# Decay tables with a per-partition factor, a merged state product, a gated first weight and a last expert by itself, in a fused RWKV and soft-MoE kernel

## The chip, the core and the metric

The kernel runs on one core of one Trainium2 chip. The metric is the device time of one execution in microseconds (us), and the median over several runs is compared. All positions in time below count from the start of the span of one profiled execution.

## What is computed

Two layers follow each other. The first is a linear attention with decay (RWKV-5): for 4 batches, 8 heads, 768 time steps and a head size of 48.

```
state = zeros(B, H, D, D)
for t in range(S):
    kt, vt, rt = k[:, :, t], v[:, :, t], r[:, :, t]
    cur = einsum('bhd,bhe->bhde', u * kt, vt)
    y[:, :, t] = einsum('bhd,bhde->bhe', rt, state + cur)
    state = w[:, :, None] * state + einsum('bhd,bhe->bhde', kt, vt)
```

Its output, as 3072 tokens of 384 features, goes through a soft mixture of 8 experts with 4 slots each (hidden size 1024):

```
logits = x @ phi                        # 3072 x 32
slot_input = softmax(logits, axis=0).T @ x
slot_out[e] = relu(slot_input[e] @ w1[e]) @ w2[e]
out = softmax(logits, axis=1) @ slot_out
```

## The kernel before, in words

**Decay.** The recurrence is turned into products of blocks of time. k and r are multiplied with tables of powers of the decay w: `W[0]` for k, `W[1]` for r, each 128 partitions x (4 head pairs q, 6 steps j, 96). An entry is exp(factor x ln w), where the factor depends on partition and j alone (`sk`, `sr`, 128 x 6) and ln w on the feature (`lnw`). `spread` (L173) copies the row w to all partitions with a matmul and takes Ln on ScalarE; `tt` (L180) multiplies `lnw` with the factor on VectorE, 576 wide; `ex` (L185) takes Exp on ScalarE. Of the four head pairs, q=0 and q=1 are made ahead of the loop (L188 to L196), q=2 and q=3 in its first steps by the table `T_AT` (L467). In the same start, GpSimd loads w and u into `wu` with two small DMAs (L107, L108), TensorE transposes it (L210), and `ucol` and `wT` come out of it (L213 to L217); nine matmuls on zeros (`keep_warm`, L137) keep TensorE busy in between.

**The loop.** The work is 16 units m (batch and head pair), each in two halves of time: 32 steps i, from -5 on with a fill (L493). The order of every engine's instructions is the order in which this loop emits them, and nothing is reordered afterwards. For one step the functions are: `a_pe` (k times r, L299) and `mask_f` (VectorE, AT, L304); `prod_f` (VectorE, L257, every second step); `y_pe` (outputs into PSUM Yb, L355 to L368) and `y_evac` (ScalarE, `x`, L375); `v_pe`/`v_evac` (v brought into order of time, L284, L290); `m_pe` (the states, into PSUM Mb, L314 to L329) and `z_evac` (VectorE: the states masked to their own head, `Z`, L343, in every even step also the state that is carried to the next half and multiplied with its decay, `Z0`, L339, and `dv`, L345); `scale` (GpSimd, the products with the decay tables, `kr`, L228, three units ahead, three buffers); `t_pe`, `t_evac` (transposes of `kr`, L235, and their ScalarE copies `kT`, `rT`, L241); `b_pe`, `b_evac` (transposed back, L247, and VectorE's copy `kn`, L252); `v_cast` (ScalarE, L270). From step 8 on `route` adds the routing of the batch before: logits (L383, L390, L399), their exponentials (L405) and the sums for the slots (L425).

**Transfers.** SP's queue carries w, then k, r and v by batch; three raw buffers hold four batches, so batch 3 is loaded into the first one again (L538). GpSimd's queue carries the expert weights, which are converted to bf16 on the way: eight of w1 (L131) and eight of w2 (L134), the last w2 in three pieces. `W_AT` (L466) says after which steps they are issued; each takes its place behind that step's GpSimd product.

**The experts.** After the loop the last two groups' logits are finished (L558 to L571), `uns` holds the slot inputs, and the first product (L594) uses four column groups of TensorE at once, one per expert. ReLU, transposes (L617) and the second product (L627) follow: for each of two expert groups g, eight blocks y, two halves x and four experts j. Its result is scaled by the column sums into `so` (L631, L632). The row sums of the second softmax (`row_sums`, L606, 24 small matmuls in all, each call with a reciprocal) stand partly ahead of, partly behind that product. Then 24 matmuls of 384 columns (L646) give the output rows, VectorE and ScalarE evacuate them in turn (L648, L650), and SP's and GpSimd's queues store them in pieces of 1, 1, 2, 4, 4, 4, 4 and 4 rows (L652).

Of the kernel before, what the change touches and what calls it, by code (L numbers as in the profile page):

```python
# [9 lines left out]
def kernel(  # L10
# [86 lines left out]
    one_f = early[0:1, 2 * H * D:2 * H * D + 128]  # L97
    warm = LexpT[:, 2048:2560]
    wu = cst.tile([8, 128], f32, name="wu")
    wu3 = wu[:].rearrange("q (e s) -> q e s", s=64)  # L100
    phi_f = cst.tile([128, nM, ES], f32, name="phi_f")
    O(act.preload_act_table_set("natural_log_exp_and_others"))
    O(sp.dma_start(out=w_row, in_=w.rearrange("(o h) d -> o (h d)", o=1)))
    O(dve.memset(wu[:], 1.0))
    O(dve.memset(warm, 0.0))
    O(dve.memset(one_f, 1.0))
    O(pool.dma_start(out=wu3[0:4, :, 0:D], in_=w.rearrange("(q e) d -> q e d", e=2)))  # L107
    O(pool.dma_start(out=wu3[4:8, :, 0:D], in_=u.rearrange("(q e) d -> q e d", e=2)))  # L108

# [7 lines left out]

    def load_batch(b, step):
        for h0 in range(0, H, step):
            load_kr(0, k, b, h0, h0 + step)  # L120
            load_kr(1, r, b, h0, h0 + step)
            load_v(b, h0, h0 + step)

    load_batch(0, 2)
    load_batch(1, 2)
    O(sp.dma_start(out=phi_f[:], in_=moe_phi.rearrange("(mo p) s -> p mo s", p=128)))
    load_batch(2, H)
# [9 lines left out]
    def keep_warm(n, bank=Yb, data=None):  # L137
        data = warm if data is None else data
        for _ in range(n):
# [4 lines left out]
    O(pool.iota(s_i, pattern=[[-1, J]], base=T - 1, channel_multiplier=-J))  # L144
    ident_f = cst.tile([128, 128], f32, name="ident_f")
    O(pool.memset(ident_f[:], 0.0))
    O(pool.affine_select(out=ident_f[:], in_=ident_f[:], compare_op=ALU.not_equal, fill=1.0, base=0,
                         pattern=[[-1, 128]], channel_multiplier=1))
# [19 lines left out]
    ident = cst.tile([128, 128], bf, name="ident")  # L168
    O(dve.tensor_copy(ident[:], ident_f[:]))

# [5 lines left out]

    spread(Xb, 0, P2)
    W = [cst.tile([128, nQ, J, P2], f32, name=f"W{j}") for j in range(2)]

# [7 lines left out]

    tt(0, 0)  # L188
    tt(1, 0)
    spread(Vb, P2, H * D)  # L190
    ex(0, 0)
    ex(1, 0)
    tt(0, 1)
    tt(1, 1)
    ex(0, 1)
    ex(1, 1)  # L196
    bmask = cst.tile([128, P2], f32, name="bmask")
    ones = cst.tile([128, 128], bf, name="ones")
    ucol = cst.tile([128, nQ, 2], bf, name="ucol")
    Le_t = [cst.tile([128, L, 128], bf, name=f"Le{j}") for j in range(2)]  # L200
    uns = cst.tile([128, nM, 2, EG, 32], bf, name="uns")
    O(pool.memset(bmask[:], 0.0))
    O(pool.memset(bmask[0:64, 0:D], 1.0))
    O(pool.memset(bmask[64:128, D:P2], 1.0))
    O(pool.memset(ones[:], 1.0))
    O(pool.memset(ucol[:], 0.0))
    for t in Le_t:
        O(pool.memset(t[:], 0.0))
    O(pool.memset(uns[:], 0.0))
    O(pe.transpose(Mb[:, 0:8], wu[:], ident_f[0:8, 0:8]))  # L210
    wuT = cst.tile([128, 8], f32, name="wuT")
    O(dve.tensor_copy(wuT[:], Mb[:, 0:8]))
    O(pool.tensor_mul(ucol[0:64, :, 0], wuT[0:64, 0:4], wuT[0:64, 4:8]))  # L213
    O(pool.tensor_mul(ucol[64:128, :, 1], wuT[64:128, 0:4], wuT[64:128, 4:8]))
    wT = cst.tile([128, nQ], f32, name="wT")
    O(act.activation(out=wT[:], in_=wuT[:, 0:4], func=AF.Ln))
    O(act.activation(out=wT[:], in_=wT[:], func=AF.Exp, scale=float(T)))  # L217
    phi_s = cst.tile([128, nM, ES], bf, name="phi_s")
    acc = cst.tile([128, NA], f32, name="acc")
    st = {}  # L220

# [110 lines left out]
    def z_evac(i):  # L332
        m, b, q, g, n = at(i)
        dv = wk.tile([128, L * 2, D], bf, name="dv", bufs=2)
        st["dv", i] = dv
        if g == 0:
            Z0 = wk.tile([128, P2], bf, name="Z0", bufs=2)
            st["Z0", m] = Z0
            O(dve.scalar_tensor_tensor(out=Z0[:], in0=Mb[:, 2 * P2:3 * P2], scalar=wT[:, q:q + 1],  # L339
                                       in1=bmask[:], op0=ALU.mult, op1=ALU.mult))  # L340
        Z = wk.tile([128, 2, P2], bf, name="Z", bufs=2)
        st["Z", i] = Z
        O(dve.tensor_mul(Z[:], Mb[:, 0:2 * P2].rearrange("p (c e) -> p c e", c=2),  # L343
                         bmask[:, None, :].to_broadcast([128, 2, P2])))
        O(dve.tensor_mul(dv[:], st["v", i][:].rearrange("p c e d -> p (c e) d"),  # L345
                         Mb[:, 288:288 + 2 * L, None].to_broadcast([128, L * 2, D])))

    def y_pe(i):
# [9 lines left out]
        for c in range(L):  # L358
            if c == 0:
                if g == 0:  # L360
                    continue
                z = st["Z0", m][:]
            else:
                z = Z[:, c - 1, :]
            t = slice((g * L + c) * C, (g * L + c + 1) * C)
            O(pe.matmul(Yb[:, c * P2:(c + 1) * P2], rT[:, t], z, start=False, stop=False,  # L366
                        skip_group_check=True))
# [24 lines left out]
    def xt_ev(n, c, xt=None, eng=None):  # L392
        xT = wk.tile([128, Dm], bf, name="xT", bufs=4)
        st["xT", n, c] = xT
        xt = xT_p if xt is None else xt
        if eng is dve:
            O(dve.tensor_copy(xT[:], xt))
        else:
            O(act.copy(xT[:], xt))  # L399
# [40 lines left out]
    def route(i, part):  # L440
# [22 lines left out]
        if s < 2 * L:  # L463
            xt_ev(*ch[s])

    W_AT = {13: 1, 14: 1, 15: 1, 16: 1, 18: 1, 19: 1, 21: 1, 22: 1, 23: 1, 25: 1, 26: 5}  # L466
    T_AT = {-4: [(dve, 0, 2), (dve, 1, 2), (act, 0, 2)], -3: [(act, 1, 2), (dve, 0, 3)],  # L467
            -2: [(act, 0, 3)], -1: [(dve, 1, 3), (act, 1, 3)]}
    nw = 0
    n0, n1 = nG - 2, nG - 1  # L470
    Wf = [t[:].rearrange("p q j d -> p (q j d)") for t in W]
    xs = Wf[0].bitcast(bf)[:, 2 * F:2 * F + 2 * L * Dm].rearrange("p (n m c t) -> p n m c t", n=2, m=nM, c=L)

# [19 lines left out]
    for i in range(-5, nH):  # L493
# [39 lines left out]
        if i == nH - 3:  # L533
            turn(n1, (0, 1), T1, act)
        for eng, j, q in T_AT.get(i, ()):
            (tt if eng is dve else ex)(j, q)
        if i == 3:
            load_batch(3, H)  # L538
        if i == 4:
            for mi in range(nM):  # L540
                O(dve.tensor_copy(phi_s[:, mi, :].rearrange("p (j g s) -> p g j s", g=2, s=Spe),
                                  phi_f[:, mi, :].rearrange("p (g j s) -> p g j s", g=2, s=Spe)))
        for _ in range(W_AT.get(i, 0)):
# [62 lines left out]
    def row_sums(a, z):  # L606
        for i in range(a, z):
            O(pe.matmul(Mb[:, i:i + 1], LexpT[:, i:Nn:nN], ones[:, 0:1],
                        start=(i == a), stop=(i == z - 1), skip_group_check=True))
        O(dve.reciprocal(rsr[:, a:z], Mb[:, a:z]))  # L610

# [3 lines left out]
    for g in range(2):  # L615
# [4 lines left out]
        if g == 0:  # L620
            row_sums(0, 8)
    SO = [Xb[:, 0:HD], Yb[:, 0:HD]]
    for g in range(2):
        for y in range(nF):
            for x in range(2):
                for j in range(EG):
                    O(pe.matmul(SO[x][32 * j:32 * j + 32, :], hT[g][:, y, 32 * j:32 * j + 32],  # L627
                                w2_of(g * EG + j)[:, y, x * HD:(x + 1) * HD],
                                start=(g == 0 and y == 0), stop=(g == 1 and y == nF - 1), skip_group_check=True))
    so = cst.tile([128, Dm], bf, name="so")  # L630
    O(dve.tensor_scalar_mul(so[:, 0:HD], SO[0], csr[:, 0:1]))  # L631
    O(act.activation(out=so[:, HD:Dm], in_=SO[1], func=AF.Copy, scale=csr[:, 0:1]))  # L632
    row_sums(8, 16)

    out_v = out.rearrange("(p n) m -> p n m", n=nN)
    ob = [T1[:].bitcast(f32), T0[:].bitcast(f32), Ab0, Vb[:], Xb[:], Yb[:]]
    sizes = [1, 1, 2, 4, 4, 4, 4, 4]
    obuf = ([raw[0][:, 16 * Dm:17 * Dm], raw[0][:, 17 * Dm:18 * Dm], Wf[0][:, 0:2 * Dm], Wf[1][:, 0:4 * Dm]]
            + [raw[0][:, x * 4 * Dm:(x + 1) * 4 * Dm] for x in range(4)])
    i = 0  # L640
    for gi, sz in enumerate(sizes):
        o_s = obuf[gi][:, 0:sz * Dm].rearrange("p (n m) -> p n m", m=Dm)
        i0 = i
        for j in range(sz):
            op = ob[i % 6][:, 0:Dm]
            O(pe.matmul(op, LexpT[:, i:Nn:nN], so[:], start=True, stop=True))  # L646
            if i % 2 == 0:
                O(dve.tensor_scalar_mul(o_s[:, j, :], op, rsr[:, i:i + 1]))  # L648
            else:
                O(act.activation(out=o_s[:, j, :], in_=op, func=AF.Copy, scale=rsr[:, i:i + 1]))  # L650
            i += 1
        O((sp, pool)[gi % 2 if gi > 1 else 0].dma_start(out=out_v[:, i0:i, :], in_=o_s))  # L652
        if gi == 2:
            row_sums(16, nN)

# [29 lines left out]
```

## Time and profile before

| | |
|---|---|
| runs | 125.37 us median of 3 (124.92 to 125.81) |
| profiled execution | 124.32 us, span 122.5 us, mean granted TensorE clock 0.967 |
| busy | TensorE 100.0, VectorE 97.3, ScalarE 84.2, GpSimd 62.5 us |
| DMA | 31.79 MB in all; mean 259 GB/s over the span |
| main loop | until about 94 us |
| first product of the experts starts | 98.27 us |
| second product | 102.54 us to 105.3 us |
| `so` complete | 105.84 us |
| first output store issued | 106.93 us |
| last GpSimd output store issued | 113.38 us |

A busy time is the sum of an engine's instructions; matmuls are pipelined and their ends modelled, so TensorE's is high without the engine being at its peak. An instruction's duration is longer than the distance to the next one's start, as neighbours overlap: two VectorE products of 0.95 us follow each other after 0.87 us. In lines of the timeline the columns are start, duration, engine, line, operation, output and inputs, count, and in brackets idle time ahead and what ended it. In lines of groups the columns after the bar are busy time and mean duration in ns, then idle time ahead.

### The profile page before, as it was taken

How to read it: one execution, taken by the hardware profiler on the slowest of the kernel's cores; microseconds unless marked ns; L12 is line 12 of the kernel's file. 1: busy time of each engine (PE TensorE's matmuls, PEld its weight loads, DVE VectorE, ACT ScalarE, POOL GpSimd, SP SyncE). 2: the span in 40 equal slices, each digit the busy share in tenths (PEclk: the TensorE clock that was granted, in tenths of full speed). 3: DMA queues.
4: the chain of work that ended last, by engine and by line, in shares of the span. 5: the costliest groups of instructions: out<-in, count | busy, mean ns of one | idle time of the engine just before them, and what ended most of it. 6: DMA issues, size and time to landing. Idle time of an engine off the chain costs nothing.

```text
span 122.5 us, 4329 instructions
## 1 busy us (share of the span) xinstructions
PE 100.0 (82%) x1784; PEld 80.5 (66%) x1785; DVE 97.3 (79%) x200; ACT 84.2 (69%) x176; POOL 62.5 (51%) x75
## 2 busy tenths in 40 slices
PE   5698988898898998989899898999979799994000
PEld 1356866686687877979778797777878549962000
DVE  1998899999999999899999999999978235598000
ACT  4479768777868798886889887788858253397000
POOL 5899999995756778494687758110000000011100
PEclk9999999999999999999999999999999999999655
DMA  2999999999999999999999999999999992069992
GB/s 66 290 372 374 372 372 366 347 388 362 328 384 372 324 217 215 212 219 212 217 218 211 220 209 215 216 217 218 215 214 215 210 193 49 5 235 395 401 415 94
DMA packets 21093, 31.79 MB, mean 259 GB/s; under 512 B 1361, under 2 KB 18258, under 8 KB 21074
## 3 DMA queue, kind: packets, MB, share of 16 engines
q0 software_dynamic: 3088, 14.95, 55.1%
q1 hardware_dynamic: 17986, 16.57, 40.1%
q8 instruction: 14, 0.23, 0.7%
q14 instruction: 5, 0.04, 0.1%
HBM read 39.38 MB, written 4.72 MB: 360 GB/s over the span
## 4 chain that ended last, share of the span: by engine, by line
DVE 38%; PE 31%; issue 11%; POOL 7%; ACT 4%; DVEq 1%; POOLq 1%; ACTq 0%
DVE prod L257 11%; DVE AT L304 8%; DVE dv L345 6%; DVE Z L343 5%; PE Vb L284 5%; DVE raw L648 3%; PE Mb L325 3%; PE Yb L368 3%; PE T L235 3%; PE T L425 2%; PE T L247 2%; POOL kr L228 2%; PE Ab L299 1%; DVE kn L252 1%; ACT W L484 1%
## 5 line engine op out<-in xcount | busy, mean ns | idle before, releaser
L228 POOL TENSOR_TENSOR kr<-raw,W 128x576 bf16<-128x576 f32 x30 | 43.2, 1459 | 14.6 <-PE T L235 11.1
L304 DVE TENSOR_TENSOR AT<-Ab,mask_ut 128x768 bf16<-128x768 f32 x32 | 30.4, 950 | 1.0 <-PE Ab L299 1.0
L284 PEld LDWEIGHTS <-Q 128*128 128x128 bf16 x288 | 16.2, 100 | 3.6 <-issue 2.9
L284 PE MATMUL Vb<-v_bf,Q 128*128 128x96 bf16 x288 | 18.2, 211 | 0.0
L235 PE MATMUL T<-ident,kr 128*128 128x128 bf16 x192 | 17.0, 230 | 0.2 <-POOL kr L228 0.2
L241 ACT COPY rT<-T 128x768 bf16<-128x768 bf16 x16 | 12.8, 798 | 6.0 <-PE T L235 2.7
L241 ACT COPY kT<-T 128x768 bf16<-128x768 bf16 x16 | 12.8, 799 | 5.1 <-PE T L235 4.8
L257 DVE TENSOR_TENSOR prod<-T,kT 128x768 bf16<-128x768 bf16 x16 | 15.1, 947 | 0.0
L375 ACT CAST x<-Yb 128x288 bf16<-128x288 f32 x32 | 13.1, 410 | 2.8 <-PE Yb L368 2.8
L652 POOL DMA_DIRECT2D out_dram<-W x1 | 0.5, 541 | 27.2 <-ACT raw L650 27.2
L345 DVE TENSOR_TENSOR dv<-vn,Mb 128x288 bf16<-128x288 bf16 x32 | 14.2, 444 | 0.0
L366 PE MATMUL Yb<-Z,rT 128*128 128x96 bf16 x80 | 10.5, 204 | 3.8 <-DVE Z L343 3.8
L290 ACT CAST vn<-Vb 128x288 bf16<-128x288 f32 x32 | 13.1, 409 | 0.5
L235 PEld LDWEIGHTS <-kr 128*128 128x128 bf16 x192 | 12.6, 102 | 1.1 <-DVE kr L228 0.5
L299 PE MATMUL Ab<-rT,kT 64*128 64x128 bf16 x192 | 11.1, 222 | 0.6 <-DVE AT L304 0.5
L325 PE MATMUL Mb<-vn,kn 128*128 128x96 bf16 (+2 forms) x80 | 11.5, 243 | 0.0
L343 DVE TENSOR_TENSOR Z<-Mb,bmask 128x192 bf16<-128x192 f32 x32 | 11.1, 347 | 0.0
L355 PE MATMUL Yb<-vn,AT 128*128 128x48 bf16 x192 | 10.3, 185 | 0.0
L368 PE MATMUL Yb<-dv,ident 128*128 128x288 bf16 x32 | 9.1, 284 | 1.4
L270 ACT CAST v_bf<-raw 128x576 bf16<-128x576 f32 x15 | 10.1, 676 | 0.0
L252 DVE COPY kn<-T 128x768 bf16<-128x768 bf16 x16 | 8.9, 555 | 1.4 <-PE T L247 0.7
L355 PEld LDWEIGHTS <-AT 128*128 128x128 bf16 x192 | 6.9, 96 | 3.2
(141 smaller groups left out, 209.4 us busy)
## 6 DMA issues: line engine op xcount, KB each, us to landing
w_all<-in_moe_w_dram POOLq DMA_DIRECT2D x8, 768.0 KB, 10.3
raw<-in_moe_w_dram POOLq DMA_DIRECT2D x7, 768.0 KB, 14.7
raw<-in_k_dram SPq DMA_DIRECT2D x8, 288.0 KB, 6.1
raw<-in_r_dram SPq DMA_DIRECT2D x8, 288.0 KB, 6.0
raw<-in_v_dram SPq DMA_DIRECT2D x8, 288.0 KB, 6.1
raw<-in_k_dram SPq DMA_DIRECT2D x2, 1152.0 KB, 10.9
raw<-in_r_dram SPq DMA_DIRECT2D x2, 1152.0 KB, 9.9
raw<-in_v_dram SPq DMA_DIRECT2D x2, 1152.0 KB, 13.1
```

The costliest lines, as they stand in the source:

```text
L228: O(eng.tensor_mul(kr[:, j].rearrange("p j (h s) -> p j h s", s=64)[:, :, :, 0:D], src, W[j][:, q].rearrange("p j (h d) -> p j h d", h=2)))
L235: O(pe.transpose(bank[:, x * C:(x + 1) * C], kr[:, j, x, :], ident[:]))
L241: O(act.copy(t[:].rearrange("p (s j) -> p s j", j=J), bank[:, 0:S].rearrange("p (j s) -> p s j", j=J)))
L257: O(dve.tensor_mul(pr[:].rearrange("p (s j) -> p s j", j=J), T1[:, 0:S].rearrange("p (j s) -> p s j", j=J), st["kT", m][:].rearrange("p (s ...
L284: O(pe.matmul(Vb[:, c * P2:(c + 1) * P2], Q3[:, o:o + C], vb[:, :, g, j, :], start=(j == 0), stop=(j == JV - 1)))
L290: O(act.copy(vn[:].rearrange("p c e d -> p (c e d)"), Vb[:, 0:L * P2]))
L304: O(dve.tensor_mul(AT[:], Ab[:, :, 0:T].rearrange("p e (c t) -> p e c t", c=L), mask_ut[:, None, None, :].to_broadcast([128, 2, L, C])))
L325: O(pe.matmul(o, kn[:, g * L + c, :], vc, start=first, stop=True, skip_group_check=True))
L343: O(dve.tensor_mul(Z[:], Mb[:, 0:2 * P2].rearrange("p (c e) -> p c e", c=2), bmask[:, None, :].to_broadcast([128, 2, P2])))
L345: O(dve.tensor_mul(dv[:], st["v", i][:].rearrange("p c e d -> p (c e) d"), Mb[:, 288:288 + 2 * L, None].to_broadcast([128, L * 2, D])))
L355: O(pe.matmul(Yb[:, o:o + D], AT[:, e, c, :], vn[:, c, e, :], start=first, stop=False, skip_group_check=True))
L375: O(act.copy(st["x", n][:, :, q * P2:(q + 1) * P2], Yb[:, 0:L * P2].rearrange("p (c e) -> p c e", c=L)))
```

## The change

- **Decay tables.** For q=0, q=2 and q=3 a new function `ad` makes a table on ScalarE alone: six Exp instructions of 128 x 96, each reading `lnw` with one column of `sk` or `sr` as its factor per partition. For q=1 the product and the Exp stay, now inside the loop's fill. The tables for q=2 and q=3 come later than before (steps -2 to 1).
- **Start.** The two small DMAs into `wu` go from GpSimd's queue to ScalarE's, ahead of its table load; `wu`'s transpose stands ahead of the second `spread`; `ucol`'s two products go from GpSimd to VectorE. Memsets of `ones` and `Le` go to step 2, that of `uns` to step 28. `ident_f` and `phi_f` lie in unused columns of `LexpT`; `xT` has two buffers for four.
- **States.** A table `zt` holds the mask for two states and, for the third, mask times decay. `Z0` is then part of `Z`: one product of 288 columns in even steps.
- **phi.** The three copies of phi go from VectorE (step 4) to ScalarE (steps 3, 4, 5).
- **Weights.** The first weights are issued in step 15 (two) for step 13 (one), behind a GpSimd copy of one column, `guard`, that reads the first part of batch 3's v; that v is loaded in two DMAs, of six heads and two.
- **Experts.** All row sums from 8 on stand ahead of the second group's product; that product is split into three experts and the last one, with two and three warm-up matmuls ahead of the parts.
- **Output.** The first two rows are evacuated in halves by both engines; the pieces are 1, 1, 2, 2, 2, 4, 4, 4 and 4 rows.

```diff
+    O(act.dma_start(out=wu3[0:4, :, 0:D], in_=w.rearrange("(q e) d -> q e d", e=2)))
+    O(act.dma_start(out=wu3[4:8, :, 0:D], in_=u.rearrange("(q e) d -> q e d", e=2)))
     O(act.preload_act_table_set("natural_log_exp_and_others"))
...
-    O(pool.dma_start(out=wu3[0:4, :, 0:D], in_=w.rearrange("(q e) d -> q e d", e=2)))
-    O(pool.dma_start(out=wu3[4:8, :, 0:D], in_=u.rearrange("(q e) d -> q e d", e=2)))
+    zt = cst.tile([128, nQ, 3, P2], f32, name="zt")
+    O(dve.memset(zt[:], 0.0))
...
+    def ad(j, q):
+        e = (sk, sr)[j]
+        for x in range(J):
+            O(act.activation(out=W[j][:, q, x, :], in_=lnw[:, q * P2:(q + 1) * P2], func=AF.Exp,
+                             scale=e[:, x:x + 1]))
+
+    ad(0, 0)
     spread(Vb, P2, H * D)
+    ad(1, 0)
...
+        O(dve.tensor_mul(Z[:], Mb[:, 0:x * P2].rearrange("p (c e) -> p c e", c=x), zt[:, q, 0:x, :]))
...
-    W_AT = {13: 1, 14: 1, 15: 1, 16: 1, 18: 1, 19: 1, 21: 1, 22: 1, 23: 1, 25: 1, 26: 5}
-    T_AT = {-4: [(dve, 0, 2), (dve, 1, 2), (act, 0, 2)], -3: [(act, 1, 2), (dve, 0, 3)],
-            -2: [(act, 0, 3)], -1: [(dve, 1, 3), (act, 1, 3)]}
+    W_AT = {15: 2, 16: 1, 18: 1, 19: 1, 21: 1, 22: 1, 23: 1, 24: 1, 25: 1, 26: 5}
+    T_AT = {-5: [(tt, 0, 1), (ex, 0, 1)], -4: [(tt, 1, 1)], -3: [(ex, 1, 1)], -2: [(ad, 0, 2)],
+            -1: [(ad, 1, 2)], 0: [(ad, 0, 3)], 1: [(ad, 1, 3)]}
...
+        if i == min(W_AT):
+            O(pool.tensor_copy(guard[:], raw_of(2, B - 1)[:, 0:1]))
...
+    second(0, range(EG))
+    row_sums(8, nN)
+    row_recip(8, nN)
+    busy(2)
+    second(1, range(EG - 1))
+    busy(3)
+    second(1, (EG - 1,))
...
-    sizes = [1, 1, 2, 4, 4, 4, 4, 4]
+    sizes = [1, 1, 2, 2, 2, 4, 4, 4, 4]
```

## The prediction

> **What bounds the kernel now.** I read the page's slices first, then DMA by windows, then VectorE, TensorE and GpSimd in order of time, and last the groups for the prices.
>
> ```profile
> DVE  1998899999999999899999999999978235598000
> ...
> DMA  2999999999999999999999999999999992069992
> GB/s 66 290 372 374 372 372 366 347 388 362 328 384 372 324 217 215 212 219 212 217 218 211 220 209 215 216 217 218 215 214 215 210 193 49 5 235 395 401 415 94
> ```
>
> Two things are full at once. VectorE is full to 90 us. DMA is full from 3 us: inputs at 370 GB/s to slice 13, then the cast weights at 215 GB/s until slice 33, a hole of four microseconds, then the output at 400 GB/s. The windows show the three joints:
>
> ```profile
> 41.50:42.00 0.50, 0.50 (x2) 1.00 1.41 351
> 42.00:42.50 0.50, 0.50 (x1) 1.00 1.03 242
> 43.50:44.00 0.50, 0.50 (x1) 1.00 1.01 210
> ...
> 103.25:103.50 0.25, 0.00 (x0) 1.00 0.04 6
> ...
> 107.75:108.00 0.25, 0.00 (x0) 1.00 0.71 264
> 108.50:108.75 0.25, 0.00 (x0) 1.00 0.07 18
> 109.00:109.25 0.25, 0.02 (x1) 1.00 1.02 362
> ```
>
> (The last two columns are DMA share and GB/s.) Inputs give way to weights at about 42.1; the last weight bytes land at 103.4; the output starts at 107.7, starves at 108.5 and is full from 109.0 to 120.25. The span ends 2.25 later, at 122.5.
>
> ```profile
> 63.98 0.45 DVE L345 TENSOR_TENSOR dv<-vn,Mb 128x288 bf16<-128x288 bf16 x1
> 64.34 0.95 DVE L304 TENSOR_TENSOR AT<-Ab,mask_ut 128x768 bf16<-128x768 f32 x1
> 65.48 0.32 DVE L339 SCALAR_TENSOR_TENSOR Z<-Mb,wT,bmask 128x96 bf16<-128x96 f32 x1 [0.19 <-PE Mb L329]
> 65.72 0.35 DVE L343 TENSOR_TENSOR Z<-Mb,bmask 128x192 bf16<-128x192 f32 x1
> 65.98 0.45 DVE L345 TENSOR_TENSOR dv<-vn,Mb 128x288 bf16<-128x288 bf16 x1
> 66.49 0.56 DVE L252 COPY kn<-T 128x768 bf16<-128x768 bf16 x1
> ```
>
> The loop takes 4.98 us for two steps. `kn` starts 0.51 after `dv`, where `dv` to AT takes 0.36: it waits 0.15 for TensorE's transposes (L247, 65.88 to 66.38). The circle is therefore dv, TensorE without a gap from 64.48 to 66.38, kn, AT, prod, Z, dv. L339 is not in it while routing (L383, L390) runs; before step 8 there is no routing and `kn` follows `dv` at 0.36 (20.97 to 21.33).
>
> ```profile
> 39.48 0.62 POOL L131 DMA_DIRECT2D w_all<-in_moe_w_dram  x1
> ...
> 42.91 1.40 POOL L228 TENSOR_TENSOR kr<-raw,W 128x576 bf16<-128x576 f32 x1 [0.36 <-PE T L235]
> 44.26 0.57 POOL L131 DMA_DIRECT2D w_all<-in_moe_w_dram  x1
> ```
>
> The first weight issues at 39.48. In the changed order it stands after the product that is here at 42.91.
>
> **The sum is against the profiled execution**: 124.32 us with a span of 122.5 (1.8 lie outside); the median of the runs is 125.37, 1.05 more, so I carry the difference over to the median.
>
> **1. Start, decay tables.** Of eight VectorE products (L182) and eight Exp (L186, 128x576), two of each stay (q=1). Six tables become six ScalarE pieces of 128x96 with a factor per partition.
>
> ```profile
> L186 ACT ACTIVATE W<-W 128x576 f32<-128x576 f32 x8 | 5.5, 685 | 1.2 <-DVE W L182 1.1
> L405 ACT ACTIVATE Le<-Xb 128x96 bf16<-128x96 f32 x6 | 1.5, 255 | 0.0
> L632 ACT ACTIVATE so<-Yb,csr 128x192 bf16<-128x192 f32 x1 | 0.4, 420 | 2.4 <-PE Yb L627 2.4
> L650 ACT ACTIVATE raw<-Vb,rsr 128x384 f32<-128x384 f32 x3 | 1.8, 609 | 0.0
> ```
>
> A piece is not in the trace. Low end: 0.14 from start to start (L405, 87.42 to 87.56, no factor). High end: its whole duration, 0.34 (0.420 of L632 less 96 columns at 0.83 ns, the slope from L632 to L650's first, 0.58). L650 repeats 0.11 sooner than its duration; I take 0.34 - 0.11 = 0.23, the rows with a factor being nearest. A table is then 6 x 0.23 = 1.4 us of ScalarE for 0.58 before.
>
> [...]
>
> VectorE loses four products of 0.67 to 0.86 between 8.7 and 17; one (16.29) stands directly on the chain between kn and AT: 0.7 gained. TensorE's `wu` transpose moves ahead of the second spread (L174) and so waits for the `wu` DMAs; behind it stand that spread, its Ln, five warm-ups and the first transposes, and on VectorE the first `kr` product. These DMAs leave GpSimd (issues of 0.74 and 0.61, landing after 3.3 and 3.8) for ScalarE's queue, at 1.05 and 1.5, ahead of the table load (1.28, then ending at 3.25, before Ln at 3.91: no cost). They land between 3.9 (2.4 after the issue, as `w_row`, issued at 0.74 and used at 3.14) and 5.3 (3.8 after); before, the wait ended at 6.07. The transpose (0.24), the spread (1.2) and five warm-ups (2.3) follow, less 0.2 of overlap: from 4.2, which I take as nearer to an empty queue, the first transposes come at 7.7 for 8.36, from 5.3 at 8.8. `zt`'s memset (1152 wide; 256 take 0.27, so 1.1) lies in VectorE's idle 1.65 before 3.05; its product (0.45) and ucol's two take the place of freed products.
>
> Then ScalarE limits. From the second kT copy (11.8: 0.9 before its 12.74) to the copy x of step 2 it has four copies of 128x768 at 0.69, two casts at 0.58, six copies of 128x288 at 0.29 and four tables at 1.4: 11.3 us, and x ends at 23.2 where it ended at 22.3. The next Yb group waits for that, and its last matmul (24.29) comes 0.24 later, at 23.45: gain 0.85. If TensorE lets kT start 0.8 earlier it is 1.65; with pieces at 0.34 it is a loss of 1.8. I take **-0.9**. GpSimd's products wait for these tables but run ahead (8 without a pause from 9.9): covered.
>
> **2. Loop.** L339 merges into L343: 0.24+0.26 start to start becomes 0.36 (as dv, 288 wide). Worth 0.09 a pair where `kn` is not held by TensorE: steps 4 to 7 (0.18) and three pairs without routing later (0.27); zero elsewhere, up to 0.14 a pair (2.2) if the circle above is wrong. Three phi copies leave VectorE (28.97 to 29.38: 0.41) for ScalarE, which idles 0.4 a step. **-0.9** together; -1.5 by step 10, -1.8 at the end. xT with two buffers, tiles in unused rows, memsets later on GpSimd (1.0): nothing, behind ScalarE's and GpSimd's idle time.
>
> **3. Weights.** The guard waits for three quarters of v, behind the first product of step 15. Half-microsecond windows from 41.0 (341, 351, 242, 277, 240 GB/s) lie between 370 for inputs and 210 for weights and hold 1.25 us of inputs: alone these would drain at 42.25, and the weights' flow amounts to a start there. Three quarters of v then land at about 41.5, with stragglers at 42.1. GpSimd comes to it at 44.26 - 1.5 = 42.75; issue at 42.9. Behind it stand two issues (1.2) and a `kr` product not needed for five steps. From issue to packets: 1.4 (output: 109.23, DMA busy from 110.65) to 2.5 (first `wu` issue 1.43, data from 3.9, GpSimd's first use, which the first weight now is). Full flow from 44.3 to 45.4 instead of 42.25. DMA was full; nothing gives this back. Last weight: 103.4 + 2.05 to 3.15, or 0.7 less if the uneven ends (100.5 to 103.4) shrink: 104.75 to 106.55, I take 106.0. The last expert alone leaves four matmuls of 0.082 after it: TensorE could end at 106.45.
>
> **4. Second product.** Before it ran from 102.54 to 105.3, 32 groups of four at 0.082. Now on TensorE's queue before its end: 16 row sums (8 in 0.52: 1.05), five warm-ups (0.21: 1.07), and the last expert's 16 matmuls by themselves (1.31; 0.33 if an expert costs its share of a group). 105.3 - 1.8 + 3.4 = **106.9**, later than the weights' 106.45. That is +1.6.
>
> **5. Output.** No row sums (0.65) or reciprocal (0.21) between so and the first row, and half rows (0.42 for 0.62): the first issue comes 0.8 after so for 1.09, gain 0.3. Five small pieces fill the hole from 108.3 to 108.95 (0.65), unless the second SP issue again takes 1.07: 0.3 to 1.0, I take **-0.95**. The remaining 4.7 MB at 400 GB/s follow unchanged.
>
> Sum: +1.6 - 0.95 = **+0.65**: 125.0 for the profiled execution, 126.0 for the median.
>
> **Rivals.**
> - *A, forecast (0.5)*: 126.0; its own range is 125.0 to 127.0.
> - *B, faster (0.23)*: TensorE gets its full rate sooner. Six transposes take 0.82 at 11.88 and 0.50 from 16.96; before, an idle gap (4.9 to 6.07) parts the warm-ups, now they run through. With 2 us more in step 1, GpSimd meets the guard as v lands and packets flow at 43.75: the last weight at 104.2, TensorE's end at 104.9, so 0.4 earlier, output -1.0: 124.0. Against it: ScalarE's 11.3 us. A loop gain of 3.7 in all decides, and the weights' uneven ends must shrink too.
> - *C, slower (0.17)*: ScalarE is the bound to step 3. Pieces at 0.28 put x at 24.4: step 1 loses 0.3, the loop's whole gain is 0.6, TensorE ends at 108.1, so +2.8 - 0.95: 127.2. It decides above 0.25 a piece. For it: no covering idle time in those 11.3 us; against: L650's repeat.
> - *D, slower (0.1)*: the first weight flows at 46.3 (GpSimd late by 1 and the 2.5): last weight 107.4, so +2.55 - 0.95: 127.0.
>
> [...]
>
> **How the numbers follow.** A measurement of this kernel tells about 1% (1.25 us) from no change. Faster is B; slower C, D and the 0.05 of A above 126.6; same the rest: 0.23, 0.45, 0.32. The range 123.8 to 127.6 leaves out under 2 in 10: B's and C's far ends.
>
> **What would show it.** ScalarE without a pause from 12 to 23 and pieces 0.23 apart (step 1); `kn` still waiting for L247's successor (2); DMA idle for 1.5 to 3 us after 42, last weight at 106 (3); no TensorE wait before the last expert (4); DMA full within 1.5 us of the first output packet (5). I am wrong if TensorE waits long for the last expert, or if the loop's end moves by 3 us or not at all.

## The result, and the profile after

The changed kernel takes 128.83 us (median of 4 runs, 128.64 to 129.2) against 125.15 for the kernel before: ratio 1.0295, 95% interval 1.0238 to 1.0351. It is slower. The profiled execution takes 128.79 us with a span of 127.0 (before 122.5). Three stretches add up to the difference:

| stretch (us) | before | after | difference | predicted |
|---|---|---|---|---|
| until the first product of the experts | 98.27 | 99.70 | +1.43 | -1.8 |
| from there to the scaling of `so` | 7.06 | 11.01 | +3.95 | +3.4 |
| from there to the end of the span | 17.17 | 16.29 | -0.88 | -0.95 |
| sum | 122.5 | 127.0 | +4.5 | +0.65 |

The profiled execution of before was 0.8 to 1.05 us below its median, that of after stands at its median. About 1 us of the +4.5 is therefore that one execution; in which line it lies, one trace of the kernel before doesn't show.

The slices of the changed kernel:

```profile
DVE  6369977779999989899898898998883350189100
...
DMA  2999999999999307999999999999999999249992
GB/s 67 303 353 374 376 370 364 361 391 352 362 384 355 90 3 114 217 215 218 217 214 215 214 214 212 211 217 215 217 216 217 216 209 203 51 170 385 403 416 112
```

DMA has a hole at slices 13 to 15, where inputs give way to weights. The windows size it (the last two columns are DMA share and GB/s), and the timeline of GpSimd says why:

```profile
43.50:48.50 5.00, 4.73 (x97) 4.02 (x94) 4.62 (x9) 4.28 (x11) 3.55 (x6) 1.00 0.00 2
49.00:50.00 1.00, 0.54 (x17) 0.43 (x14) 1.00 (x3) 0.86 (x2) 1.00 (x2) 1.00 0.46 80
109.25:109.50 0.25, 0.25 (x4) 0.24 (x4) 0.00 (x0) 0.00 (x0) 0.00 (x0) 1.00 0.13 19
...
113.00:113.25 0.25, 0.25 (x2) 0.09 (x1) 0.25 (x2) 0.25 (x2) 0.00 (x0) 1.00 0.99 344
```

```profile
27.66 16.45 POOL L227 TENSOR_TENSOR kr<-raw,W 128x576 bf16<-128x576 f32 x12
44.28 1.41 POOL L227 TENSOR_TENSOR kr<-raw,W 128x576 bf16<-128x576 f32 x1 [0.18 <-PE T L234]
45.63 0.19 POOL L546 COPY guard<-raw 128x1 f32<-128x1 f32 x1
47.08 1.28 POOL L137 DMA_DIRECT2D w_all<-in_moe_w_dram  x2 [1.26 <-issue]
```

GpSimd had lost its lead: it runs twelve products without a pause up to 44.1 and comes to the guard at 45.63. The first weight flows at 48.5, and in full from 50 on (before 42.25), the last bytes land at 109.4 (before 103.4).

The second product on TensorE, from the last products of its first group on:

```profile
105.22 0.26 PE L637 MATMUL Yb<-raw,W 128*32 128x192 bf16 x4
105.41 1.28 PE L614 MATMUL Mb<-ones,LexpT 128*128 128x1 bf16 x16
106.55 0.59 PE L146 MATMUL Ab<-w_all 128*128 128x512 bf16 x2
107.07 0.26 PE L637 MATMUL Xb<-raw,W 128*32 128x192 bf16 x3
...
108.51 0.82 PE L146 MATMUL Ab<-w_all 128*128 128x512 bf16 x3
109.26 0.26 PE L637 MATMUL Xb<-raw,W 128*32 128x192 bf16 x1
...
110.51 0.25 PE L637 MATMUL Yb<-raw,W 128*32 128x192 bf16 x1
```

No line has idle time ahead of it: TensorE works through, and no wait for a weight shows. Sixteen row sums, five warm-ups and a last expert that costs as much as the three others together (1.33 us each) stand in its queue.

The steady loop, where routing runs, is unchanged:

```profile
65.36 0.44 DVE L341 TENSOR_TENSOR dv<-vn,Mb 128x288 bf16<-128x288 bf16 x1
65.72 0.95 DVE L303 TENSOR_TENSOR AT<-Ab,mask_ut 128x768 bf16<-128x768 f32 x1
66.86 0.46 DVE L340 TENSOR_TENSOR Z<-Mb,zt 128x288 bf16<-128x288 f32 x1 [0.19 <-PE Mb L328]
67.24 0.44 DVE L341 TENSOR_TENSOR dv<-vn,Mb 128x288 bf16<-128x288 bf16 x1
67.87 0.56 DVE L251 COPY kn<-T 128x768 bf16<-128x768 bf16 x1 [0.18 <-PE T L246]
...
70.33 0.44 DVE L341 TENSOR_TENSOR dv<-vn,Mb 128x288 bf16<-128x288 bf16 x1
```

Two steps take 4.97 us (before 4.98), and `kn` still waits for TensorE. The loop's +1.43 arises between the `dv` of step 2 (21.03 for 20.97) and that of step 4 (27.34 for 25.79). There ScalarE makes the tables of q=2 and q=3, six pieces a table (`ad`, L200), and TensorE waits three times for the copies `x` behind them, 2.57 us in all:

```profile
13.49 0.80 ACT L240 COPY kT<-T 128x768 bf16<-128x768 bf16 x1 [0.90 <-PE T L234]
...
20.76 1.72 ACT L200 ACTIVATE W<-LexpT,sk 128x96 f32<-128x96 f32 x6
22.36 0.40 ACT L371 CAST x<-Yb 128x288 bf16<-128x288 f32 x1
...
25.23 0.41 ACT L371 CAST x<-Yb 128x288 bf16<-128x288 f32 x1
```

```profile
19.37 0.31 PE L351 MATMUL Yb<-vn,AT 128*128 128x48 bf16 x6 [0.58 <-ACT x L371]
22.81 0.31 PE L351 MATMUL Yb<-vn,AT 128*128 128x48 bf16 x6 [1.11 <-ACT x L371]
25.68 0.31 PE L351 MATMUL Yb<-vn,AT 128*128 128x48 bf16 x6 [0.88 <-ACT x L371]
```

Up to step 2, what the freed products bring is used up: the first transposes come at 9.30 (before 8.36), and VectorE's new product for `zt` stands ahead of the first `kn` (before 11.02):

```profile
10.67 1.77 DVE L535 TENSOR_TENSOR zt<-zt,wT 128x384 f32<-128x384 f32 x1
12.36 0.55 DVE L251 COPY kn<-T 128x768 bf16<-128x768 bf16 x1
```

### The profile page after: what moved, and what is told of

The parts are those of the page before. It is cut to its first block, busy times and chain, and to the rows that moved or that the text cites. A ratio compares the mean times of both kernels' runs of the same rounds, so it can differ in the third digit from the quotient of the medians.

```text
span 127.0 us, 4336 instructions
## 1 busy us (share of the span) xinstructions
PE 101.7 (80%) x1792; PEld 80.7 (64%) x1792; DVE 94.0 (74%) x180; ACT 89.3 (70%) x210; POOL 59.6 (47%) x70
## 4 chain that ended last, share of the span: by engine, by line
PE 32%; DVE 28%; ACT 17%; issue 9%; DMA 5%; ACTq 1%; POOLq 0%; DVEq 0%
DVE prod L256 10%; DVE AT L303 10%; ACT W L200 6%; PE Vb L283 4%; DVE dv L341 3%; PE T L246 3%; DMA wu<-in_u_dram 3%; PE T L234 3%; PE Yb L364 3%; PE Mb L324 2%; DVE Z L340 2%; PE T L421 2%; DMA out_dram<-W 2%; PE Xb L637 2%; ACT x L371 2%
## 5 line engine op out<-in xcount | busy, mean ns | idle before, releaser
L227 POOL TENSOR_TENSOR kr<-raw,W 128x576 bf16<-128x576 f32 x30 | 42.1, 1418 | 16.6 <-PE T L234 5.6
L283 PEld LDWEIGHTS <-Q 128*128 128x128 bf16 x288 | 15.6, 98 | 4.1 <-issue 3.3
L283 PE MATMUL Vb<-v_bf,Q 128*128 128x96 bf16 x288 | 17.5, 206 | 0.8 <-ACT vn L289 0.8
L234 PE MATMUL T<-ident,kr 128*128 128x128 bf16 x192 | 16.5, 224 | 1.5 <-DVE kn L251 1.0
L340 DVE TENSOR_TENSOR Z<-Mb,zt 128x288 bf16<-128x288 f32 (+1 forms) x32 | 12.9, 402 | 4.1 <-PE Mb L328 4.1
L341 DVE TENSOR_TENSOR dv<-vn,Mb 128x288 bf16<-128x288 bf16 x32 | 14.2, 443 | 0.0
```

The costliest lines, as they stand in the source:

```text
L227: O(eng.tensor_mul(kr[:, j].rearrange("p j (h s) -> p j h s", s=64)[:, :, :, 0:D], src, W[j][:, q].rearrange("p j (h d) -> p j h d", h=2)))
L234: O(pe.transpose(bank[:, x * C:(x + 1) * C], kr[:, j, x, :], ident[:]))
L283: O(pe.matmul(Vb[:, c * P2:(c + 1) * P2], Q3[:, o:o + C], vb[:, :, g, j, :], start=(j == 0), stop=(j == JV - 1)))
L340: O(dve.tensor_mul(Z[:], Mb[:, 0:x * P2].rearrange("p (c e) -> p c e", c=x), zt[:, q, 0:x, :]))
```

## The experiments

All ratios are to runs of the kernel before, taken beside it on the same chip; 1% is 1.25 us.

| kernel | ratio | interval |
|---|---|---|
| changed kernel | 1.0295 | 1.0238 to 1.0351 |
| e1: no warm-ups | 1.0236 | 1.0183 to 1.0290 |
| e2: early weights | 1.0270 | 1.0203 to 1.0338 |
| e3: e2, second product undivided, no warm-ups | 1.0114 | 1.0074 to 1.0154 |
| e4: changed kernel, old tables | 1.0408 | 1.0359 to 1.0457 |
| e5: e3, old start and old tables | 1.0120 | 1.0058 to 1.0182 |
| e6: e3, old start | 1.0046 | 1.0020 to 1.0072 |
| e7: e3, old tables for q=2, 3 | 1.0178 | 1.0130 to 1.0226 |
| e8: e5, row sums in the output | 1.0098 | 1.0056 to 1.0139 |
| e9: before, new loads of w and u | 1.0155 | 1.0091 to 1.0219 |
| e10: before, new tables | 1.0232 | 1.0205 to 1.0258 |
| e11: e12, q=3 tables on VectorE | 0.9974 | 0.9925 to 1.0022 |
| e12: e6, row sums spread over the output | 1.0007 | 0.9973 to 1.0041 |
| e13: e10, phi on ScalarE | 0.9988 | 0.9954 to 1.0022 |
| e14: changed kernel, phi on VectorE | 1.0631 | 1.0571 to 1.0691 |
| e15: e11, zt's product on GpSimd | 0.9926 | 0.9885 to 0.9968 |

In six of the profiled executions (e5, e7, e8, e9, e10, e14) the granted TensorE clock falls to 0.50 for a while between 12 and 42 us; in the others, the kernel before and the changed one among them, no slice ahead of the output is under 0.9. Where a reading below could rest on that, it says so. A profile of e5 is also 1.3 us above its median (127.14 for 125.84).

**The second product: late weights (theory W) or TensorE's own queue (theory Q)?** e1 takes the warm-ups out, e2 issues the weights as before, e3 also leaves the second group undivided:

```diff
-    busy(2)
-    second(1, range(EG - 1))
-    busy(3)
-    second(1, (EG - 1,))
+    second(1, range(EG))
...
-    W_AT = {15: 2, 16: 1, 18: 1, 19: 1, 21: 1, 22: 1, 23: 1, 24: 1, 25: 1, 26: 5}
+    W_AT = {13: 1, 14: 1, 15: 1, 16: 1, 18: 1, 19: 1, 21: 1, 22: 1, 23: 1, 25: 1, 26: 5}
...
-            O(pool.tensor_copy(guard[:], raw_of(2, B - 1)[:, 0:1]))
```

> The changed kernel without the five warm-up matmuls between the parts of the second product. Theory Q (TensorE's own queue sets the end of the second product: it ran from 103.98 to 110.77 without a pause, the last weight landed at 109.45): the warm-ups lie on the path, but after 0.8 to 0.9 us the last weight binds, so 128.8 becomes 128.0. Rival W (the late weights set the end, the warm-ups only fill a wait): no change, 128.8.

> The changed kernel without the guard and with the weights issued after the same steps as before the change (first one after step 13). The DMA hole from 42.5 to 49.5 should nearly close and the last weight should land at 104 to 105 instead of 109.45. Theory Q: the end does not move, 128.8 (within 0.3). Rival W: 5 us earlier at the weights, and so at least 3 us less, 125.5.

> As the run with early weights, and the second group's product in one piece again, without warm-ups (the row sums stay ahead of it). Theory Q: 1.07 of warm-ups and 1.31 of the last expert by itself go, 2.4 less: 126.4. Rival W: no more than the run with early weights gives. This run also prices the division: if an expert by itself costs its share of a group only, 1.1 to 1.4 less instead of 2.4.

e2 shortens the time in which DMA is nearly idle (a share under 0.1) from 5.5 us (43.0 to 48.5) to 1.0, the last weight lands at 105 instead of 109.4, and the time stays: W falls for this kernel. e3 brings 2.3 us to the changed kernel and 2.0 to e2, where Q worked out 2.4. In e1 the late weights show at once: inside the last expert two of the groups come 0.62 and 0.30 us late, 0.46 us of it a wait for a piece of w2. So of the 1.4 us that the warm-ups take in the changed kernel, 0.5 is left as a gain in the trace, and 0.7 by the ratio.

**The start and the tables: ScalarE's pieces (theory S) or the late w and u (theory L)?** "Old start" puts the two small loads on GpSimd's queue, `wu`'s transpose behind the second spread, and `ucol` on GpSimd. "Old tables" are `tt` and `ex` in their old places.

```diff
-    O(act.dma_start(out=wu3[0:4, :, 0:D], in_=w.rearrange("(q e) d -> q e d", e=2)))
-    O(act.dma_start(out=wu3[4:8, :, 0:D], in_=u.rearrange("(q e) d -> q e d", e=2)))
+    O(pool.dma_start(out=wu3[0:4, :, 0:D], in_=w.rearrange("(q e) d -> q e d", e=2)))
+    O(pool.dma_start(out=wu3[4:8, :, 0:D], in_=u.rearrange("(q e) d -> q e d", e=2)))
...
-    T_AT = {-5: [(tt, 0, 1), (ex, 0, 1)], -4: [(tt, 1, 1)], -3: [(ex, 1, 1)], -2: [(ad, 0, 2)],
-            -1: [(ad, 1, 2)], 0: [(ad, 0, 3)], 1: [(ad, 1, 3)]}
+    T_AT = {-4: [(tt, 0, 2), (tt, 1, 2), (ex, 0, 2)], -3: [(ex, 1, 2), (tt, 0, 3)], -2: [(ex, 0, 3)],
+            -1: [(tt, 1, 3), (ex, 1, 3)]}
```

> The changed kernel with all decay tables made as before (a VectorE product and one Exp of 576 columns each, in the old places); the small loads on ScalarE's queue, the early transpose and all else stay. Theory S (24 pieces at 0.267 make ScalarE the bound of steps 1 to 3): VectorE's dv of step 3 comes 1.3 to 1.8 us earlier than in the changed kernel (24.92) and the whole loop with it; GpSimd reaches the guard as much earlier: 127.2. Rival L (the late landing of the small loads on ScalarE's queue, and TensorE's late start behind them, lose the time): dv of step 3 moves by less than 0.4 and the time stays at 128.5 or above.

> Built on the kernel with early weights and an undivided second product (126.4). Only the four tables that are made inside the loop's first steps (q=2 and q=3) go back to one VectorE product and one Exp of 576 columns, in steps -4 to -1; q=0 stays in pieces, and the start of w and u stays the changed one. It takes 24 pieces at 0.267 us (6.4 us) off ScalarE and gives it four Exp of 0.58 (2.3 us). Theory S expects x(1) to end at about 20.5 instead of 22.8 and 125.0 in all. Theory L expects 126.4.

> Built on the kernel with early weights and an undivided second product (126.4). Only the start of w and u is the old one: small loads on GpSimd's queue, transpose behind the second spread, ucol on GpSimd. The tables stay as in the changed kernel (six ScalarE pieces each for q=0, 2 and 3). Theory S expects no gain, 126.4, with TensorE still waiting some 2.5 us for the copies x. Theory L expects the loss back, 125.1.

> Built on the kernel with early weights and an undivided second product (126.4). In addition the start is the old one: the two small loads of w and u on GpSimd's queue, wu's transpose behind the second spread, all eight decay tables by VectorE's product and one Exp of 576 columns, in their old places. What stays of the change: the merged state product with zt, phi on ScalarE, later memsets, row sums ahead of the second group, finer output. Theory S (the ScalarE pieces are the loop's +1.4) and theory L (the late landing of w and u with the earlier transpose is it) both expect the loop's whole loss back and the merge's and phi's gain of 0.3: 124.6 to 124.8. If it stays above 125.5, the loop's loss has a cause that neither names.

Without the pieces the kernel gets slower, not faster (e4 +1.4 us to the changed kernel, e7 +0.8 to e3). What S describes is real: e7 goes from the `dv` of step 2 to that of step 4 in 4.73 us, e3 with its waits for `x` in 6.31. But the old tables cost more ahead of it (first `kn` of e7 at 13.74 for 12.48, `dv` of step 2 at 23.41 for 21.15), so S falls as a reason for the loss. e7's clock is at 0.50 from 15.3 to 18.7; the 1.26 us at the first `kn` lie ahead of that, the rest isn't told apart from it. The old start gives back 0.85 us (e3 to e6), with the waits for `x` still there (0.59, 1.11 and 0.88): L holds, smaller than expected. e5 lands above 125.5, where neither names the cause. Its VectorE shows it, beside GpSimd's products from 9.90 on (second fence); the clock falls only at 20.8:

```profile
8.67 0.74 DVE L187 TENSOR_TENSOR W<-LexpT,sk 128x576 f32<-128x576 f32 x1
9.34 1.21 DVE L187 TENSOR_TENSOR W<-LexpT,sr 128x576 f32<-128x576 f32 x1
10.47 1.76 DVE L540 TENSOR_TENSOR zt<-zt,wT 128x384 f32<-128x384 f32 x1
...
12.62 1.49 DVE L187 TENSOR_TENSOR W<-LexpT,sk 128x576 f32<-128x576 f32 x1
...
16.96 1.77 DVE L187 TENSOR_TENSOR W<-LexpT,sr 128x576 f32<-128x576 f32 x1
18.65 0.94 DVE L308 TENSOR_TENSOR AT<-Ab,mask_ut 128x768 bf16<-128x768 f32 x1
```

```profile
9.90 8.21 POOL L232 TENSOR_TENSOR kr<-raw,W 128x576 bf16<-128x576 f32 x5
```

The same product of 576 takes 0.74 us before 9.90 and up to 1.77 after it, and `zt`'s of 384, priced at 0.45 in the prediction, 1.76: the first `kn` comes behind it at 12.15 (before 11.02). AT, which reads PSUM, keeps its 0.94. This gave theory G: VectorE's instructions that read only SBUF wait for GpSimd's.

**Each part alone, in the kernel before.** e9 takes the new loads and the early transpose, e10 the new tables (`ad` and `T_AT` as in the change).

> The kernel before with one part of the change alone: the two small loads of w and u on ScalarE's queue ahead of its table load, and wu's transpose ahead of the second spread. Everything else as before. Theory L (this start is late by itself): dv of step 0 comes 0.8 to 2.7 us later than at 15.13, and the median is 0.7 to 1.4 above before. The prediction's step 1 took this part as a gain (first transposes at 7.7 instead of 8.36): 0.3 to 0.6 below before.

> The kernel before with another part alone: the tables of q=0, 2 and 3 in ScalarE pieces, at the places and steps of the changed kernel; start of w and u, state products and everything else as before. Theory S (pieces are the loss): TensorE waits three times for the copies x, 2.5 us in all, and the median is 1.0 to 1.5 above before. Theory T (a trade: ScalarE's pieces cost some 2 us between steps 1 and 4, and VectorE's four products that are gone bring as much ahead of step 2): within 0.4 of before, with dv of step 2 earlier by 0.6 or more and dv of step 4 within 0.5. The prediction's step 1 expected 0.5 to 0.9 below before.

e9 loses 1.55% (1.9 us, more than L's 0.7 to 1.4). Its transpose waits for `u` until 6.10, and the second spread, which stood at 3.67, comes behind it. The first `kn` is 1.5 us late (12.54 for 11.02), ahead of the fall of the clock (14.2 to 17.6):

```profile
6.10 0.24 PE L178 MATMUL Mb<-ident_f,wu 8*128 8x8 f32 x1 [2.23 <-DMA wu<-in_u_dram]
6.20 1.30 PE L174 MATMUL Vb<-LexpT 1*128 1x288 f32 x2
```

e10 misses both theories, S and T. Starts of `dv` by step:

| step | before | changed | e9 | e10 | e13 | e15 |
|---|---|---|---|---|---|---|
| 0 | 15.13 | 15.01 | 17.01 | 14.10 | 14.49 | 14.12 |
| 2 | 20.97 | 21.03 | 23.02 | 20.75 | 20.44 | 20.65 |
| 4 | 25.79 | 27.34 | 27.85 | 26.36 | 26.76 | 25.39 |
| 6 | 30.73 | 32.18 | 32.80 | 33.87 | 31.61 | 30.12 |
| 8 | 35.55 | 36.91 | 37.61 | 38.68 | 36.44 | 34.85 |
| 31 | 93.97 | 95.33 | 96.03 | 97.09 | 94.86 | 93.31 |

Up to step 4 e10 is 0.6 behind; between 4 and 6 it loses 2.6 more, at a clock of 1.00 (it was at 0.50 from 18.6 to 22.0). The three phi copies stand there. First and second fence: VectorE and GpSimd in the kernel before; third and fourth: the same two in e10.

```profile
28.97 0.48 DVE L541 CAST phi_s<-phi_f 128x32 bf16<-128x32 f32 x3
```

```profile
9.90 19.35 POOL L228 TENSOR_TENSOR kr<-raw,W 128x576 bf16<-128x576 f32 x13
```

```profile
29.57 3.02 DVE L541 CAST phi_s<-phi_f 128x32 bf16<-128x32 f32 x3
```

```profile
24.32 12.33 POOL L228 TENSOR_TENSOR kr<-raw,W 128x576 bf16<-128x576 f32 x9 [1.46 <-ACT W L191]
```

Two of the three copies take 1.44 us each in e10, about the length of one GpSimd product (1.41). In the kernel before, GpSimd's first long run of products ends at 29.25, just as the copies come.

**Theory G tried.**

```diff
-            for mi in range(nM):
-                O(dve.tensor_copy(phi_s[:, mi, :].rearrange("p (j g s) -> p g j s", g=2, s=Spe),
+        if 3 <= i < 3 + nM:
+            O(act.copy(phi_s[:, i - 3, :].rearrange("p (j g s) -> p g j s", g=2, s=Spe),
```

This is e13's edit to e10; e14 makes the reverse edit to the changed kernel. e15 turns one word (`dve.tensor_mul(zt` to `pool.tensor_mul(zt`).

> The kernel before with the new tables (1.023 by itself), and in addition the three phi copies on ScalarE in steps 3 to 5 as in the changed kernel. Theory G (VectorE's instructions that read and write only SBUF wait for GpSimd's products, and the late tables have put GpSimd's products where these copies stand: 3.02 us for three copies of 128x32 instead of 0.41 before): the ratio falls by 2.4 to 2.7 us, to 1.003. If the phi copies only cost their 0.41, the ratio stays at 1.020.

> The changed kernel with one part undone: the three phi copies go back to VectorE in step 4. The prediction priced this part at 0.41, so 129.2 for 128.8. Theory G: GpSimd's products run without a pause from 27.7 to 44.1 in the changed kernel, the copies (due at about 31) wait for one product each, and the time rises by 2 to 2.6, to 131.

> The best candidate (old start of w and u, new tables for q=0 and q=2, VectorE tables for q=3, early weights, undivided second product, row sums spread over the output; 0.997 by itself) with the product that puts the decay into zt moved from VectorE, where it took 1.75 us for 384 columns beside GpSimd's products, to GpSimd itself, ahead of its first product. Theory G: the first kn starts some 0.3 us sooner and VectorE's products around it are not stretched; 0.3 to 0.8 us less, ratio 0.991 to 0.995. If the product was hidden anyway: 0.997.

e13 is 2.4% (3 us) faster than e10: G holds, against a price of 0.41. e14 is 4.2 us slower than the changed kernel, more than expected: the copies take 3.88 us and steps 6 to 9 lose a further 1.3. There the clock has fallen: TensorE stands idle for 3.00 us until the late AT (35.84), the granted clock is 0.50 from 35.0 to 41.8, and nine matmuls (L283) take 0.93 for 0.54. In e10 TensorE was idle for 2.15 us at that place, and the clock stayed at 1.00.

```profile
31.05 3.88 DVE L544 CAST phi_s<-LexpT 128x32 bf16<-128x32 f32 x3
...
PEclk9999999999756999999999999999999999999755
```

(The last line is e14's granted clock in 40 slices of 3.3 us, in tenths.)

So the tables in ScalarE pieces, together with phi on ScalarE, make no difference that can be measured (e13, 0.9988); without phi on ScalarE they cost 2.9 us.

**Row sums.** e8 calls `row_sums` and `row_recip` for 8 to 15 behind the third output piece and for 16 to 23 behind the fifth; e12 and e11 put four behind the product and two behind each of rows 4 to 9. In e11 the tables of q=3 are `tt` and `ex` in steps -1 to 1.

```diff
     second(0, range(EG))
-    row_sums(8, nN)
-    row_recip(8, nN)
     second(1, range(EG))
+    row_sums(8, 12)
...
+            if 4 <= i < 10:
+                for x in range(4 + 2 * i, 6 + 2 * i):
+                    row_sums(x, x + 1)
```

> The first kernel of this call (old start and old tables, early weights, undivided second product) with the 16 later row sums moved behind the third and the fifth output piece, where TensorE has idle time beside the output DMA. It tells whether the row sums ahead of the second group are on the path. If TensorE's own queue sets the end of the second product, 1.0 to 1.28 us go: 123.4 for 124.6. If the output starves for them, the gain is under 0.5.

> The same without the mix: old start of w and u, new tables, early weights, undivided second product, and the 16 later row sums behind it (four beside the scaling of so, two after each of the output rows 4 to 9). Theory Q (TensorE's own queue sets the end of the second product, and its idle time in the output is free): 125.3 less 1.1 to 1.28 = 124.1. If the output starves for the sums again, 124.9.

> A candidate: the kernel with the old start of w and u, new tables, early weights and undivided second product (125.3), with the 16 later row sums taken out of the second product: four right behind it, beside the scaling of so, and two after each of the output rows 4 to 9. In addition the tables of q=3 go back to VectorE products and whole Exps (steps -1 to 1), so that ScalarE has 12 pieces less in the loop's first steps while VectorE waits there anyway. Row sums: 1.1 us less than 125.3. Mix: if ScalarE's load between steps 1 and 4 is what holds x, another 0.5 to 1.0 goes: 123.2 to 123.7. If VectorE's products stretch beside GpSimd's as in the old tables, nothing goes: 124.2.

The second product is 1.3 us shorter without them (e8: 2.57 for 3.89 from its first to its last group), but the output then starves. In e12:

```profile
108.00:108.50 0.50, 0.50 (x8) 0.48 (x7) 0.50 (x2) 0.50 (x2) 0.00 (x0) 1.00 0.78 289
108.50:109.00 0.50, 0.50 (x7) 0.49 (x6) 0.50 (x2) 0.48 (x1) 0.00 (x0) 1.00 0.31 92
109.00:109.50 0.50, 0.50 (x5) 0.46 (x5) 0.50 (x2) 0.50 (x2) 0.47 (x1) 1.00 0.24 89
109.50:110.00 0.50, 0.50 (x4) 0.38 (x3) 0.50 (x3) 0.50 (x3) 0.09 (x1) 1.00 1.08 390
```

TensorE is busy throughout and DMA waits for rows: by the ratios 0.3 us (e5 to e8, both with the clock's fall) and 0.5 (e6 to e12) are left of the 1.3, and neither difference is clear of its intervals. The mix of e11 is within e12's interval. e15 is faster than the changed kernel and, by 0.7%, than the kernel before (0.9926): its first `kn` starts 4.95 us after `wu`'s transpose, where e6, e11 and e12 have 5.20. Its VectorE products of 576 in steps -1 and 0 take 0.75 each, as in e11: GpSimd idles beside the first and begins after the start of the second. Its gain over e11 (0.5%) isn't clear of the two intervals, which overlap; that over the kernel before is.

## Why the prediction was wrong, by its own steps

By the ratios, the divided product with its warm-ups (1.8%, e3), the start of w and u (0.7%, e6) and the row sums (0.4%, e12) make up the loss: e12, without them and with early weights, is at 1.0007, so the rest of the change nets to nothing. The prediction had the first and the last in its +3.4. What failed is the loop: it forecast -1.8 there, and the traces show +1.43, part of which may be the one execution of the kernel before.

- **Step 1, the start (-0.9 with the tables): wrong.** It took the landing of w and u at 4.2, "nearer to an empty queue", and the first transposes at 7.7. The transpose came at 5.86 and the first transposes at 9.30, past the far end that it gave (8.8). By itself this part costs 1.55% (e9), and 0.85 us in the changed kernel. Behind it, `zt`'s product took 1.77 us for the 0.45 that was priced, beside GpSimd's first product (10.28 to 12.01). So ScalarE's second `kT` copy came at 13.49, not at 11.8, and `x` of step 2 ended at 25.64, not at 23.2. Of these 2.4 us, 1.7 are this late begin and 0.8 the pieces: ScalarE's sum from there took 12.15 us for 11.3.
- **Step 1, the tables: size and conclusion wrong.** A piece takes 0.267 us (next instruction 1.60 us after six begin), not 0.23. The choice by the nearest rows was wrong. Rival C's point (0.25 a piece) was passed and its waits came. Yet the pieces are not the loss: what they cost by step 4, VectorE's freed products give back ahead of it (e10: step 0 at 14.10 for 15.13, step 4 at 26.36 for 25.79; with phi on ScalarE no difference is left, e13 at 0.9988). The predicted gain is what is missing.
- **Step 1, "GpSimd's products run ahead: covered": wrong.** It read eight products without a pause from 9.9; the trace has thirteen, to 29.25. Late tables took this lead away, and GpSimd then ran without a pause through steps 4 to 11, close up to the guard, and where phi's copies stay on VectorE (e10, e14), into these.
- **Step 2 (-0.9): the circle right, phi wrong.** With routing, the merge is worth nothing, as said (4.97 for 4.98). Of the 0.9, 0.2 came: from the `dv` of step 4 to that of step 31 the changed kernel takes 67.99 us for 68.18. The phi copies were priced by their 0.41 in the kernel before. Beside GpSimd's products they cost 3 us (e10 to e13) or more (e14), so moving them was a condition for the new tables, not a small gain.
- **Step 3: the wait right, its size wrong, and harmless.** Guard at 45.63 (predicted 42.75), first flow at 48.5 (44.3 to 45.4, rival D 46.3), last weight 109.4 (106.0). As TensorE's own end moved by 5.3, nothing waits that the trace shows (e2); with the warm-ups gone it does (e1).
- **Step 4 (+3.4): right, 0.55 short.** Measured 3.95: row sums 1.25 (1.05), warm-ups 0.52 and, with the gap ahead of them, 0.86 (1.07 together), last expert 1.33 (1.31).
- **Step 5 (-0.95): right**, -0.88.

By the traces the sum misses by 3.85: 3.23 in the loop, 0.55 in step 4, 0.07 in step 5. The carry to the median takes 1.05 of it back, which leaves 128.83 against 126.0. Rival B's quicker TensorE came (six transposes L246 in 0.51 at 11.04, before 0.82 at 10.09; the granted clock reads 1.00 at both, so that the clock is the reason is not shown), but TensorE's next work then waits 1.03 us for VectorE's `kn`, behind `zt`'s product.

## What to carry to other kernels

Price an instruction by the company that it will have after the change: one on VectorE that works in SBUF alone can take as long as the GpSimd product beside it (a phi copy took 1.44 us in e10, beside products of 1.41, and 0.17 in the kernel before). When an engine that was ahead loses its lead, everything "covered" by that lead has to be priced anew. Before splitting or padding a matmul chain, add up what stands in its own queue until its end; a late transfer matters only if it ends after that.

## What the runs showed of the hardware

- VectorE and GpSimd held each other up where VectorE's operands lay only in SBUF: a product of 576 took 0.74 (before, at 4.49) to 1.97 us (e7, at 10.71), one of 384 0.55 (e7) or 1.77 (changed kernel), two `kr` products 1.41 (before) or 3.76 (e4), three casts of 32 columns 0.48 (before) or 3.88 (e14). GpSimd's product of 1.41 took 1.91 beside them (e10, at 9.24). Instructions that read PSUM kept their times in these kernels (AT 0.94 to 0.96). The 1.44 of two phi copies in e10 agrees with one product of 1.41; by what the one engine holds up the other, no run here shows.
- Two loads of 1.5 KB on ScalarE's queue, issued from 1.01 and 2.29 on (changed kernel), were little earlier than on GpSimd's (1.43 and 2.16, before): `wu`'s transpose came at 5.58 (e4), 5.86 (changed kernel) and 6.10 (e9), on GpSimd's queue at 6.07 (before), 6.29 (e10), 6.35 (e6) and 6.43 (e5).
- A lone column group on TensorE cost as much as three or four side by side: in the changed kernel 0.083 us from one to the next with four (103.98 to 105.22), with three (107.07 to 108.32) and with one (109.26 to 110.51).
- The granted clock of TensorE fell to 0.50 in six profiled executions, among them from 14.2 to 17.6 in e9, 15.3 to 18.7 in e7, 18.6 to 22.0 in e10 and 35.0 to 41.8 in e14. Near the fall TensorE had stood idle, for 3.00 us at a stretch in e14, 2.00 in e7, 1.75 in e5 and 1.20 in e9; in e10 for 0.81 (until 15.69) and 0.59 (until 18.27). After a stretch of 2.15 in e10 (until 33.51) there was no fall, so the length of one such stretch alone doesn't settle it.
- GpSimd's first weight came 1.26 us after the guard's end in the changed kernel (guard 45.63, issue 47.08) with nothing that the profile shows; with old tables (e4) it came at once (guard 47.15, issue 47.27). This was not explained.
